# Attention in front of two dense stages: six conversion steps for a weight slice, one bank for the tail keys

## The chip, the cores and the metric

The kernel runs on one core of a Trainium2 chip. The metric is the device time of one launch in microseconds (us): the median of three runs, with the lowest and the highest. One further execution was recorded by the hardware profiler; every row below comes from that one.

The names of the engines are those of the profile. PE is the matrix engine (PEld its weight loads), DVE the vector engine, ACT the scalar engine, POOL the GpSimd engine, SP the queue that issues most DMAs. PE writes its results into PSUM, which has eight banks of 128 partitions by 2 KB; the other engines read them from there and write to SBUF.

## The reference

Attention over 2 batches x 8 heads, 576 rows of 64 elements, then two dense stages on its output. All in float32.

```
q_rot, k_rot = rotate(q), rotate(k)
scores = q_rot @ k_rot.T / sqrt(64)
scores = scores - max(scores, axis=-1)
attn = exp(scores)
attn = attn / (sum(attn, axis=-1) + 1e-09)
x = attn @ v                                # (1152, 512) after the heads are joined
h = x @ w_in;  x = (h * sigmoid(h)) @ w_out # 512 -> 2048 -> 512
...                                         # then four experts, 512 -> 1024 -> 512
```

The 1e-09 in the divisor is the guard that the change touches.

## The kernel before

A float32 number is carried as two halves, a high and a low one, each of a type that PE multiplies exactly; a product of two numbers is two or three matmuls that add up in one bank. So nearly every result of PE is read twice: ACT copies the high half, DVE subtracts it from the bank to get the low half.

**Attention** goes through 8 pairs of heads, and each pair through 9 steps, numbered 0 to 8: eight units of 128 rows of one head, and in step 8 a tail unit of the last 64 rows of both heads. The work is pipelined over steps. In a step the scores (L383, and L388 to L395 for the tail) and row maxima (L402) are those of the unit two steps on, the exponentials (L412, which also add up the row's sum) those of the next one, and the transposes (T, L288) those of the present one. The transposed exponentials leave the bank as a high half (ACT, L452) and a low half (DVE, L457).

Each pair's rows are cut into two halves: half 0 holds 256 rows, half 1 holds 320 rows with the tail. When all units of a half are transposed, its product with V follows, one for each head: P0 and P1 for half 0 of the present pair, L0 and L1 for half 1 of the pair before (nine matmuls each, L490). A product leaves its bank by an ACT copy (tmp, L500) and a DVE addition (xu, L502). The divisor of the half is made on DVE when its last unit is transposed: L466 adds the guard to the sums, L468 takes the reciprocal. POOL spreads it (L510, L515), PE transposes it (Pn and Ln, L288 reading rb), and DVE multiplies (xn, L543). xn is split into halves by ACT and POOL (xh L538, xl L539) when the next step has its "X".

512 of the 576 keys of a unit are transposed into a bank of four 128-wide blocks. The other 64 keys, the **tail keys**, of both heads of a row block are transposed together into a second bank, and ACT copies them out (L454): 128 wide for each row block, 64 wide for the tail unit. The tail unit's block is made by way of a matrix pr: ACT copies two 64x64 blocks to its diagonal (L417), and one matmul against two stacked unit matrices puts them in place (L448).

**The order is written by hand.** A table gives, for each step, the order of atoms: S scores, M row maximum, T transposes, v the ACT side and V the DVE side of the results waiting in banks, E exponentials, H and L the high and low half of the step's transposes, X the split of xn, B the background. A second table says which background a step holds: step 0 has Nk (the transposes of the next pair's keys) and L0, step 2 Nq0 and L1, step 3 Ln, step 4 P0, step 7 Nq1 and P1, step 8 Pn. Pairs 0, 6 and 7 have tables of their own. At the end of a step POOL and then the conversion of weights get their turn.

**Banks.** Four one-bank buffers (pool ps1, by the function bank) serve in turn for transposes, products, normalisers and keys alike: a new tile waits until the last reader of the bank that it gets is done. Scores have two tiles of two banks each.

**Weight slices.** While attention runs, four slices of the first weight matrix are converted from 64-bit to two 32-bit halves (widen, L81). Each goes in three stages at the ends of three steps that follow one another: s0 (ACT L88, DVE L89 and L90), s1 (DVE L94 to L96), s2 (ACT L100, DVE L101 and L102). With the table of starts, s0 falls to step 7 of pairs 1, 2, 3 and 5, s1 to step 8, and s2 to step 0 of the next pair.

After attention come the dense stages, three matmuls for every product, from about 190 us to the end. The change doesn't touch them.

Of the kernel before, what the change touches and what calls it, by code (L numbers as in the profile page):

```python
# [30 lines left out]
def f32(ap):  # L31
    return ap.bitcast(F32)
# [3 lines left out]
def fused_kernel(ctx, tc, q, k, v, w_in, w_out, dprobs, w1, w2, cst, out):  # L36
# [43 lines left out]

    def widen(cv, raw, wh, wl):  # L81
        lw, hw = (raw.rearrange("p (n a) -> p n a", a=2)[:, :, a] for a in range(2))
# [14 lines left out]

        def s2():
            t = T["t"]
            nc.scalar.copy(wh, f32(t))  # L100
            V.tensor_scalar(hw, t[:], 0xFF800000, None, ALU.bitwise_and)  # L101
            V.scalar_tensor_tensor(wl, lw, 2.0 ** -43, f32(hw), ALU.mult, ALU.mult)  # L102

        return [s0, s1, s2]

# [38 lines left out]
    cv0 = apool(lctx, "cv0", 2, "left")  # L144
    ps1 = actx.enter_context(tc.tile_pool(name="ps1", bufs=4, space=bass.MemoryType.PSUM, side="right"))
    psS = ectx.enter_context(tc.tile_pool(name="psS", bufs=2, space=bass.MemoryType.PSUM))

    PR = hold5.tile([128, 128], F32, name="pr")
    V5 = [hold5.tile([128, 2, 128], F32, name=f"v5_{i}") for i in range(2)]
# [212 lines left out]
    def prep_small(P):  # L362
        P.nm = sp.tile([128, 10], F32, name="nm")
        P.sm = sp.tile([128, 10], F32, name="sm")
        P.rs = sp.tile([128, 10], F32, name="rs")
        P.pt, P.xu, P.tmp, P.rb = {}, {}, {}, {}
        P.s = {}
# [36 lines left out]
    def expo(P, un):  # L404
# [3 lines left out]
        if h != 1:  # L408
# [3 lines left out]
        nc.scalar.activation(o.rearrange("p (a b) -> p a b", a=2), s[:, :, 0:288], AF.Exp,  # L412
                             bias=P.nm[:, c:c + 1], scale=1.0, accum_out=P.sm[:, c:c + 1])
        if r == 4:
            for a in range(2):
                rows = slice(64 * a, 64 * a + 64)
                nc.scalar.copy(PR[rows, 64 * a:64 * a + 64], o[rows, 512:576])  # L417

    def transp(P, un):
        hf, r, h = un  # L420
        if (r, h) == (P.halves[hf][0], 0):
# [4 lines left out]
                pool.tile([128, W], F32, name="p5"),  # L426
            )
        pth, ptl, pt5 = P.pt[hf]
        ps = bank(512)
# [5 lines left out]
        five = h > 0  # L435
        W5 = 64 if h == 2 else 128
        if r < 4:
            src = ps.rearrange("p (j c) -> p j c", j=4)
            hi, lo = pth[:, h, :, o:o + 128], ptl[:, h, :, o:o + 128]
            if five:  # L440
                p5 = bank(128)
                tr(p5, pr[:, 512:640])
        else:
            src = ps.rearrange("p (j h c) -> p j h c", j=4, h=2)
            hi = pth[:, :, :, o:o + 64].rearrange("p h j c -> p j h c")
            lo = ptl[:, :, :, o:o + 64].rearrange("p h j c -> p j h c")
            p5 = bank(64)
            nc.tensor.matmul(p5, PR[:], idn2, start=True, stop=True)  # L448
        last = un == [u for u in P.units if u[0] == hf][-1]

        def high():
            nc.scalar.copy(hi, src)  # L452
            if five:
                nc.scalar.copy(pt5[:, o:o + W5], p5)  # L454

        def low():
# [8 lines left out]
            for a, b in rng:  # L465
                nc.vector.tensor_scalar(P.rs[:, a:b], P.sm[:, a:b], 1e-9, None, ALU.add)  # L466
            for a, b in rng:
# [490 lines left out]
    def attention():  # L958
# [27 lines left out]
        def slice0(t):  # L986
            raw = stg0.tile([128, 1024], U32, name="raw0")
            nc.sync.dma_start(raw[:], units[0][:, t, :])
            return widen(cv0, raw, wslot[0][0][:, t, :], wslot[0][1][:, t, :])

        for t in range(FT):
            feed.add(0, lambda t=t: slice0(t))
        nc.vector.memset(PR[:], 0.0)
        yk = pp.tile([128, 1152], F32, name="p", tag="p").rearrange("p (a e d) -> p a e d", e=2, d=64)
# [34 lines left out]
        for i in range(2):  # L1029
            g.memset(V5[i][:], 0.0)  # L1030
            g.memset(f32(QR[i][:]), 0.0)
            g.memset(f32(KH[i][:, 1152:1184]), 0.0)
            g.memset(f32(KL[i][:, 1152:1184]), 0.0)
# [230 lines left out]
```

## Time and profile before

| what | value |
|---|---|
| median of three runs | 786.53 us (784.13, 788.88, 786.53) |
| profiled execution | 786.0 us, of which the span 784.2 us |
| mean granted clock of PE | 0.990 of full speed |
| PE busy | 749.6 us, 96% of the span |
| DVE busy | 528.9 us, 67% |
| ACT busy | 354.6 us, 45% |
| attention | about 0 to 187 us |

PE is busy nearly all the time over the whole program; in attention DVE and ACT are near their limit too, so that what decides there must be read stretch by stretch. "Turn of a pair" below means steps 8, 0 and 1, where the last half of one pair and the first units of the next meet.

### The profile page before, as it was taken

To read this page: it belongs to the slowest core of one execution; us is meant where nothing else is said; L and a number is where in the kernel's file an instruction comes from. 1 tells how busy PE (TensorE), PEld (TensorE's weight loads), DVE (VectorE), ACT (ScalarE), POOL (GpSimd) and SP (SyncE) were. 2 spreads that over 40 slices of the span, in tenths; PEclk is the share of its full clock that TensorE was granted. 3 is DMA by queue.
4 is the path that set the end of the run, shared out by engine and by line. 5 is a ranking of instruction groups with operands and counts; after the bars stand their busy time and mean duration, and the time that the engine had idled before them with its cause. 6 is when DMAs were issued, how large, how long until landed. Compare 5 with 4: busy or idle time off the path is not lost.

```text
span 784.2 us, 12135 instructions
## 1 busy us (share of the span) xinstructions
PE 749.6 (96%) x4576; PEld 695.1 (89%) x4576; DVE 528.9 (67%) x964; ACT 354.6 (45%) x853; POOL 298.7 (38%) x319
## 2 busy tenths in 40 slices
PE   3899889999999999999969999999999999999998
PEld 3888789899999999999969898988989889898996
DVE  5789998987999899894894454544545454354542
ACT  3788888896534425234443141322423234142320
POOL 7877677421001303104871523516134160432500
PEclk9899999999999999999989999999999999999999
DMA  4444444140313133131100110301103021020002
GB/s 125 119 127 120 114 103 112 34 139 8 108 55 108 54 111 105 55 116 46 54 26 30 42 66 1 108 1 55 55 0 109 0 57 52 3 106 1 1 28 94
DMA packets 30986, 51.89 MB, mean 66 GB/s; under 512 B 7168, under 2 KB 13968, under 8 KB 30928
## 3 DMA queue, kind: packets, MB, share of 16 engines
q1 hardware_dynamic: 28800, 50.06, 20.8%
q10 hardware_dynamic: 2000, 0.77, 0.4%
q8 instruction: 36, 0.59, 0.3%
q0 software_dynamic: 128, 0.28, 0.1%
q14 instruction: 22, 0.18, 0.1%
HBM read 41.40 MB, written 2.36 MB: 56 GB/s over the span
## 4 chain that ended last, share of the span: by engine, by line
PE 84%; DVE 9%; ACT 3%; issue 1%; POOL 1%; DMA 1%; SPq 0%; ACTq 0%; DVEq 0%
PE m L805 9%; PE m L807 9%; PE m L806 9%; PE m L732 7%; PE m L734 7%; PE m L733 7%; PE b L288 5%; PE m L628 4%; PE m L630 4%; PE m L629 4%; PE b L490 4%; PE m L652 4%; PE m L651 4%; PE m L653 4%; PE s L383 3%; DVE ptl L457 1%
## 5 line engine op out<-in xcount | busy, mean ns | idle before, releaser
L811 DVE SCALAR_TENSOR_TENSOR acc<-m,dp,acc 128x512 f32<-128x512 f32 (+1 forms) x64 | 47.5, 743 | 112.3 <-PE m L807 112.3
L806 PE MATMUL m<-wl,gh 128*128 128x512 f32 (+1 forms) x292 | 114.5, 392 | 0.0
L807 PE MATMUL m<-wh,gl 128*128 128x512 f32 (+1 forms) x292 | 114.5, 392 | 0.0
L805 PE MATMUL m<-wh,gh 128*128 128x512 f32 (+1 forms) x292 | 114.5, 392 | 0.0
L753 DVE SCALAR_TENSOR_TENSOR gl<-g,gh 128x288 fp32r<-128x288 f32 x96 | 57.0, 593 | 49.1 <-ACT gh L752 48.6
L715 POOL TENSOR_TENSOR wl<-raw,wh 128x512 fp32r<-128x512 f32 x24 | 31.1, 1296 | 143.0 <-ACT wh L712 143.0
L640 POOL TENSOR_TENSOR gl<-g,gh 128x384 fp32r<-128x384 f32 x24 | 26.9, 1122 | 142.7 <-ACT gh L639 142.6
L732 PE MATMUL m<-xh,wh 128*128 128x288 f32 x256 | 76.3, 298 | 0.0
L733 PE MATMUL m<-xl,wh 128*128 128x288 f32 x256 | 75.9, 296 | 0.0
L734 PE MATMUL m<-xh,wl 128*128 128x288 f32 x256 | 75.9, 296 | 0.0
L715 POOL TENSOR_TENSOR wl<-cvt,wh 128x512 fp32r<-128x512 f32 x32 | 41.8, 1308 | 74.0 <-ACT wh L712 74.0
L652 PE MATMUL m<-gh,wl 128*128 128x384 f32 (+1 forms) x208 | 67.2, 323 | 0.0
L653 PE MATMUL m<-gl,wh 128*128 128x384 f32 (+1 forms) x208 | 67.2, 323 | 0.0
L651 PE MATMUL m<-gh,wh 128*128 128x384 f32 (+1 forms) x208 | 67.2, 323 | 0.0
L807 PEld LDWEIGHTS m<-wh,gl 128*128 128x128 f32 x292 | 54.9, 188 | 12.9
L805 PEld LDWEIGHTS m<-wh,gh 128*128 128x128 f32 x292 | 54.9, 188 | 11.8
L806 PEld LDWEIGHTS m<-wl,gh 128*128 128x128 f32 x292 | 54.9, 188 | 11.8
L288 PE MATMUL b<-cs,p 128*128 128x128 f32 x329 | 52.0, 288 | 13.8 <-ACT p L1008 7.6
L732 PE MATMUL m<-tf,wh 128*128 128x288 f32 x192 | 57.5, 299 | 6.7 <-DVE g L787 5.6
L712 ACT CAST wh<-cvt 128x512 fp32r<-128x512 f32 x32 | 19.9, 621 | 96.3 <-DVE cvt L711 96.3
L752 ACT ACTIVATE gh<-g 128x288 fp32r<-128x288 f32 x96 | 42.9, 447 | 33.6 <-DVE g L787 19.0
L734 PE MATMUL m<-tf,wl 128*128 128x288 f32 x192 | 57.4, 299 | 0.0
(175 smaller groups left out, 2127.9 us busy)
## 6 DMA issues: line engine op xcount, KB each, us to landing
raw<-in_moe_w_dram SPq DMA_DIRECT2D x16, 1024.0 KB, 5.1
raw<-in_moe_w_out_dram SPq DMA_DIRECT2D x8, 1024.0 KB, 5.0
raw<-in_moe_w_in_dram SPq DMA_DIRECT2D x6, 1024.0 KB, 5.2
kh<-kkh SPq DMA_DIRECT2D x28, 128.0 KB, 2.8
kl<-kkl SPq DMA_DIRECT2D x28, 128.0 KB, 2.4
xv<-in_v_dram SPq DMA_DIRECT2D x8, 256.0 KB, 2.8
raw<-in_moe_w_in_dram SPq DMA_DIRECT2D x4, 512.0 KB, 3.9
xk<-in_k_dram SPq DMA_DIRECT2D x7, 256.0 KB, 2.9
```

What stands on the lines that cost most here:

```text
L288: nc.tensor.matmul(o, lhsT, idn[:, 0:n], is_transpose=True, start=True, stop=True)
L651: nc.tensor.matmul(o, wh[:, f, ds], gh[:, cols], start=(f == 0), stop=False)
L652: nc.tensor.matmul(o, wl[:, f, ds], gh[:, cols], start=False, stop=False)
L653: nc.tensor.matmul(o, wh[:, f, ds], gl[:, cols], start=False, stop=(f == FT - 1))
L715: nc.gpsimd.tensor_tensor(lo, src(name), f32(hi), ALU.subtract)
L732: nc.tensor.matmul(ps, wh[:, k, ms], hh[:, k, cols], start=(first and k == 0), stop=False, skip_group_check=not first)
L733: nc.tensor.matmul(ps, wh[:, k, ms], hl[:, k, cols], start=False, stop=False, skip_group_check=not first)
L734: nc.tensor.matmul(ps, wl[:, k, ms], hh[:, k, cols], start=False, stop=(k == 1), skip_group_check=not first)
L753: nc.vector.scalar_tensor_tensor(lo, src, 0.0, f32(hi), ALU.max, ALU.subtract)
L805: nc.tensor.matmul(ps, gh[:, ts], wh[:, f, ds], start=(f == 0), stop=False)
L806: nc.tensor.matmul(ps, gh[:, ts], wl[:, f, ds], start=False, stop=False)
L807: nc.tensor.matmul(ps, gl[:, ts], wh[:, f, ds], start=False, stop=(f == FT - 1))
```

## The change

It has four parts.

1. **Six stages for a slice instead of three.** With slow=True, widen gives an empty stage, s0, s1, an empty stage, the ACT cast (L100 before, L99 after) and the two DVE steps of s2 (L101 and L102 before, L103 and L104 after) apart. So s0 goes from step 7 to step 8, s1 from step 8 to step 0, the ACT cast from step 0 to step 2, and the two last DVE steps from step 0 to step 3.
2. **Tail keys of a half in one bank.** ps1 has three banks, and a new pool ps5 has one, in which the tail-key transposes of a half lie side by side. One ACT copy for a half, of 256 or 320 columns, takes the place of the copy for each row block.
3. **The guard as a column of the sums.** The sums get a second column that holds 1e-09 from the start, and a reduction over two columns on DVE takes the place of the addition.
4. **The tail block is transposed in place.** pr and its ACT copies go; two 64x64 matmuls put the blocks straight into the bank of ps5.

```diff
-    def widen(cv, raw, wh, wl):
+    def widen(cv, raw, wh, wl, slow=False):
...
         def s2():
+            nc.scalar.copy(wh, f32(T["t"]))
+
+        def s3():
             t = T["t"]
-            nc.scalar.copy(wh, f32(t))
             V.tensor_scalar(hw, t[:], 0xFF800000, None, ALU.bitwise_and)
             V.scalar_tensor_tensor(wl, lw, 2.0 ** -43, f32(hw), ALU.mult, ALU.mult)
 
-        return [s0, s1, s2]
+        if slow:
+            return [lambda: None, s0, s1, lambda: None, s2, s3]
+        return [s0, s1, lambda: (s2(), s3())]
...
-    ps1 = actx.enter_context(tc.tile_pool(name="ps1", bufs=4, space=bass.MemoryType.PSUM, side="right"))
+    ps5 = actx.enter_context(tc.tile_pool(name="ps5", bufs=1, space=bass.MemoryType.PSUM, side="right"))
+    ps1 = actx.enter_context(tc.tile_pool(name="ps1", bufs=3, space=bass.MemoryType.PSUM, side="right"))
...
-    PR = hold5.tile([128, 128], F32, name="pr")
+    SM = [hold5.tile([128, 10, 2], F32, name=f"sm_{i}") for i in range(2)]
...
-                             bias=P.nm[:, c:c + 1], scale=1.0, accum_out=P.sm[:, c:c + 1])
-        if r == 4:
-            for a in range(2):
-                rows = slice(64 * a, 64 * a + 64)
-                nc.scalar.copy(PR[rows, 64 * a:64 * a + 64], o[rows, 512:576])
+                             bias=P.nm[:, c:c + 1], scale=1.0, accum_out=P.sm[:, c, 0:1])
...
+            P.ps5 = ps5.tile([128, 512], F32, name="b5")
...
-            p5 = bank(64)
-            nc.tensor.matmul(p5, PR[:], idn2, start=True, stop=True)
+            for a in range(2):
+                rows = slice(64 * a, 64 * a + 64)
+                nc.tensor.matmul(p5[rows, :], pr[rows, 512:576], idn[rows, rows], start=True, stop=True)
...
-            if five:
-                nc.scalar.copy(pt5[:, o:o + W5], p5)
+            if last:
+                nc.scalar.copy(pt5[:], P.ps5[:, 0:P.W[hf]])
...
-                nc.vector.tensor_scalar(P.rs[:, a:b], P.sm[:, a:b], 1e-9, None, ALU.add)
+                nc.vector.tensor_reduce(P.rs[:, a:b], P.sm[:, a:b, :], AX.X, ALU.add)
...
-            return widen(cv0, raw, wslot[0][0][:, t, :], wslot[0][1][:, t, :])
+            return widen(cv0, raw, wslot[0][0][:, t, :], wslot[0][1][:, t, :], True)
...
+            g.memset(SM[i][:], 1e-9)
```

**PE at the turn from pair 1 to pair 2.** In order: the transposes of the tail unit T8, the tail-key block, Pn (reading rb), T0 (reading p), Nk (reading yk), L0 (reading pth and V), T1 with its tail keys. Before:

```order
L288 MATMUL b_814<-cs_61,p_802 128x128 x4
L448 MATMUL b_819<-cs_61,pr_111 128x64
L288 MATMUL b_832<-cs_61,rb_716 128x128 x2
L288 MATMUL b_857<-cs_61,p_826 128x128 x4
L288 MATMUL b_872<-cs_61,yk_645 128x128 x4
L490 MATMUL b_877<-pth_683,V_530 128x320
L288 MATMUL b_912<-cs_61,p_826 128x128 x4
L288 MATMUL b_917<-cs_61,p_826 128x128
```

And in the changed kernel:

```order
L293 MATMUL b_798<-cs_61,p_792 128x128 x4
L450 MATMUL b5_680<-cs_61,p_792 64x64 x2
L293 MATMUL b_816<-cs_61,rb_711 128x128 x2
L293 MATMUL b_843<-cs_61,p_810 128x128 x4
L293 MATMUL b_858<-cs_61,yk_640 128x128 x4
L492 MATMUL b_863<-pth_677,V_526 128x320
L293 MATMUL b_898<-cs_61,p_810 128x128 x4
L293 MATMUL b5_842<-cs_61,p_810 128x128
```

The order of PE's work is the same; the banks differ. Before, every line takes the next of four banks, so T1 (b_912) gets that of Pn (b_832) and L0 (b_877) that of T8 (b_814). In the changed kernel the tail keys are out of the round, and the lines named b take the next of three banks: L0 (b_863) gets that of Pn (b_816), T1 (b_898) that of T0 (b_843), Nk (b_858) that of T8 (b_798).

**DVE at the same turn.** xu is the addition behind P1, ptl the low half of T8 and then of T0, rs the divisor, nm a row maximum, xn the multiplication that reads the bank of Pn; raw0 and cvt are the weight slice. Before:

```order
L90 SCALAR_TENSOR_TENSOR raw0_767<-raw0_767 128x512
L502 TENSOR_TENSOR xu_704<-b_792,tmp_705 64x256
L402 TENSOR_REDUCE nm_778<-s_821 128x1
L457 TENSOR_TENSOR ptl_684<-b_814,pth_683 128x4x2x64
L466 TENSOR_SCALAR rs_480<-sm_479 128x5
L468 RECIPROCAL rs_480<-rs_480 128x5
L94 TENSOR_SCALAR cvt_808<-cvt_808 128x512
L95 TENSOR_SCALAR cvt_808<-cvt_808 128x512
L96 SCALAR_TENSOR_TENSOR cvt_808<-raw0_767,cvt_808 128x512
L402 TENSOR_REDUCE nm_778<-s_864 128x1
L543 TENSOR_TENSOR xn_862<-xu_704,b_832 128x256
L457 TENSOR_TENSOR ptl_855<-b_857,pth_854 128x4x128
```

And in the changed kernel:

```order
L504 TENSOR_TENSOR xu_699<-b_782,tmp_700 64x256
L407 TENSOR_REDUCE nm_769<-s_805 128x1
L459 TENSOR_TENSOR ptl_678<-b_798,pth_677 128x4x2x64
L468 TENSOR_REDUCE rs_478<-sm_1_115 128x5
L470 RECIPROCAL rs_478<-rs_478 128x5
L89 TENSOR_SCALAR raw0_760<-raw0_760 128x512
L90 SCALAR_TENSOR_TENSOR raw0_760<-raw0_760 128x512
L407 TENSOR_REDUCE nm_769<-s_850 128x1
L545 TENSOR_TENSOR xn_848<-xu_699,b_816 128x256
L459 TENSOR_TENSOR ptl_840<-b_843,pth_839 128x4x128
L94 TENSOR_SCALAR cvt_835<-cvt_835 128x512
L95 TENSOR_SCALAR cvt_835<-cvt_835 128x512
```

L89 and L90 now stand between the divisor and xn, where L94 to L96 stood; these stand behind the low half of T0, where L101 and L102 stood. At a turn without a slice none of the raw0 and cvt rows is there.

**DVE at step 3 of the pair that follows.** The same names; xn here is that of Ln. Before:

```order
L457 TENSOR_TENSOR ptl_855<-b_979,pth_854 128x4x128
L466 TENSOR_SCALAR rs_780<-sm_779 128x4
L468 RECIPROCAL rs_780<-rs_780 128x4
L543 TENSOR_TENSOR xn_1013<-xu_878,b_986 128x320
L402 TENSOR_REDUCE nm_778<-s_1014 128x1
```

And in the changed kernel:

```order
L459 TENSOR_TENSOR ptl_840<-b_964,pth_839 128x4x128
L468 TENSOR_REDUCE rs_770<-sm_0_114 128x4
L470 RECIPROCAL rs_770<-rs_770 128x4
L103 TENSOR_SCALAR raw0_760<-cvt_835 128x512
L104 SCALAR_TENSOR_TENSOR wl0_65<-raw0_760 128x512
L545 TENSOR_TENSOR xn_1000<-xu_864,b_970 128x320
L407 TENSOR_REDUCE nm_769<-s_1001 128x1
```

The last two steps of the slice now stand ahead of xn. On ACT the cast of the slice now stands at the end of step 2, behind the exponentials and ahead of the copy of L1's product.

## Rows read from the trace of the kernel before

**Rows 1.** Part 1 of the page: busy us (share of the span) and instructions.

```profile
PE 749.6 (96%) x4576; PEld 695.1 (89%) x4576; DVE 528.9 (67%) x964; ACT 354.6 (45%) x853; POOL 298.7 (38%) x319
```

**Rows 2.** Windows: tail scores to tail scores, with a slice, then without; busy us (count).

```profile
97.30:119.58 22.28, 20.16 (x146) 18.10 (x145) 21.15 (x38) 18.99 (x50) 15.91 (x19) 1.00 0.40 103
119.58:139.63 20.05, 19.55 (x144) 18.02 (x144) 16.79 (x31) 17.83 (x49) 15.30 (x20) 1.00 0.43 112
```

**Rows 3.** Timeline, turn 4 to 5 (no slice): start, duration, engine, line, operation.

```profile
127.10 0.53 DVE L466 TENSOR_SCALAR rs<-sm 128x5 f32<-128x5 f32 x1
127.33 0.39 PE L490 MATMUL b<-pth,V 128*128 128x320 f32 x1
...
127.77 0.72 DVE L402 TENSOR_REDUCE nm<-s 128x1 f32<-128x576 f32 x1
...
128.41 0.41 DVE L543 TENSOR_TENSOR xn<-xu,b 128x256 f32<-128x256 f32 x1
...
129.32 0.42 ACT L500 COPY tmp<-b 64x320 f32<-64x320 f32 x1 [0.53 <-PE b L490]
...
129.77 0.74 ACT L412 ACTIVATE p<-s,nm 128x576 f32<-128x576 f32 x1
```

**Rows 4.** Timeline, turn 3 to 4 (with a slice).

```profile
101.72 1.00 DVE L89 TENSOR_SCALAR raw<-raw 128x512 uint32<-128x512 uint32 x1
...
102.76 0.69 DVE L90 SCALAR_TENSOR_TENSOR raw<-raw 128x512 uint32<-128x512 uint32 x1
...
105.62 0.39 PE L490 MATMUL b<-pth,V 128*128 128x320 f32 x1
...
108.21 0.62 ACT L100 CAST wh<-cvt 128x512 fp32r<-128x512 f32 x1 [1.61 <-DVE cvt L96]
...
108.77 0.41 DVE L543 TENSOR_TENSOR xn<-xu,b 128x256 f32<-128x256 f32 x1
...
109.32 0.90 PE L288 MATMUL b<-cs,p 128*128 128x128 f32 x5 [1.21 <-DVE xn L543]
...
109.34 0.42 ACT L500 COPY tmp<-b 64x320 f32<-64x320 f32 x1
...
109.79 0.74 ACT L412 ACTIVATE p<-s,nm 128x576 f32<-128x576 f32 x1
```

**Rows 5.** The divisor's line L466 over all 16: duration in ns, lowest/median/highest.

```profile
L466 DVE TENSOR_SCALAR rs<-sm x16: 157/571/979, 29.5 to 186.7; 128x4 f32<-128x4 f32 x8, 128x5 f32<-128x5 f32 x8
```

**Rows 6.** Timeline, steps 0 to 4 of pair 4: slice's last steps, L1's copy, xn.

```profile
109.70 0.41 DVE L101 TENSOR_SCALAR raw<-cvt 128x512 uint32<-128x512 uint32 x1
...
110.15 0.69 DVE L102 SCALAR_TENSOR_TENSOR wl<-raw 128x512 fp32r<-128x512 uint32 x1
...
114.17 0.42 ACT L500 COPY tmp<-b 64x320 f32<-64x320 f32 x1 [0.32 <-PE b L490]
...
117.30 0.46 DVE L543 TENSOR_TENSOR xn<-xu,b 128x320 f32<-128x320 f32 x1
...
117.79 0.46 ACT L538 CAST xh<-xn 128x320 fp32r<-128x320 f32 x1 [0.28 <-DVE xn L543]
```

**Rows 7.** Timeline, turn 5 to 6 (with a slice).

```profile
151.20 0.33 PE L288 MATMUL b<-cs,p 128*128 128x128 f32 x1 [1.08 <-DVE ptl L457]
```

**Rows 8.** Timeline, pair 0, behind its first divisor.

```profile
31.68 0.74 ACT L412 ACTIVATE p<-s,nm 128x576 f32<-128x576 f32 x1 [1.07 <-DVE nm L402]
```

**Rows 9.** Groups by line, 30 to 280 us: the copies that go; busy us, mean ns.

```profile
L454 ACT COPY p<-b 128x128 f32<-128x128 f32 (+1 forms) x38 | 10.1, 266 | 0.0
...
L417 ACT COPY pr<-p 64x64 f32<-64x64 f32 x16 | 3.9, 244 | 0.3
```

**Rows 10.** Windows in pair 0: PE busy first, granted clock third from last.

```profile
19.40:22.20 2.80, 0.66 (x4) 0.42 (x4) 2.80 (x4) 0.83 (x3) 2.63 (x3) 0.87 0.51 141
22.20:25.00 2.80, 2.75 (x12) 2.73 (x13) 1.84 (x3) 1.74 (x5) 2.80 (x4) 0.50 0.06 12
25.00:28.30 3.30, 3.30 (x17) 3.27 (x17) 2.54 (x4) 2.28 (x7) 3.22 (x5) 0.50 0.74 223
```

More of the change, by code (lines that the diff above doesn't have):

```diff
@@ L363, in prep_small @@
         P.nm = sp.tile([128, 10], F32, name="nm")
-        P.sm = sp.tile([128, 10], F32, name="sm")
+        P.sm = SM[P.i]
         P.rs = sp.tile([128, 10], F32, name="rs")
@@ L435, in transp @@
         five = h > 0
-        W5 = 64 if h == 2 else 128
+        p5 = P.ps5[:, o:o + (64 if h == 2 else 128)]
         if r < 4:
@@ L440, in transp @@
             if five:
-                p5 = bank(128)
                 tr(p5, pr[:, 512:640])
@@ L988, in slice0 @@
             nc.sync.dma_start(raw[:], units[0][:, t, :])
-            return widen(cv0, raw, wslot[0][0][:, t, :], wslot[0][1][:, t, :])
+            return widen(cv0, raw, wslot[0][0][:, t, :], wslot[0][1][:, t, :], True)
         for t in range(FT):
             feed.add(0, lambda t=t: slice0(t))
-        nc.vector.memset(PR[:], 0.0)
         yk = pp.tile([128, 1152], F32, name="p", tag="p").rearrange("p (a e d) -> p a e d", e=2, d=64)
```

## The prediction

> **What bounds the kernel now.** I read the busy table first. PE is busy 96% of the span [rows 1], so over the whole program there is little to win but PE's idle time, and the change removes no large piece of PE's work. Then I cut attention into windows of one pair each, from tail scores to tail scores. A pair without a weight slice takes 20.05 us with PE busy 19.55, so PE sets it. A pair with a slice takes 22.28 us with PE busy 20.16, DVE 21.15 and ACT 18.99 [rows 2]: the 2.23 us more are PE waiting, and DVE is nearly full. Everything that the change touches lies there, so I read the turn of a pair instruction by instruction, without a slice [rows 3] and with one [rows 4].
>
> At the turn with a slice PE starts L0 at 105.62 and then stops 1.21 us at T1, because T1's bank is the one that xn of Pn still reads [rows 4]. xn is late because L94 to L96 stand ahead of it on DVE. Without a slice T1 doesn't wait: L0 starts at 127.33, xn runs 128.41 to 128.82, and T1 comes later than that [rows 3].
>
> **Part by part: the banks.** With three banks in the round instead of four it is L0, and no longer T1, that gets the bank of Pn, so L0 waits for xn. L0 is nine matmuls earlier in PE's order than T1, and in before it started ahead of xn at either kind of turn. Queued behind L0 on PE are the scores of step 0's unit and T1; behind them wait the copy of L0's product on ACT and the next exponential, which stand in order.
>
> Turn without a slice (0 to 1 and 4 to 5). The divisor gets shorter (below) by 0.53 - 0.16 = 0.37, so xn ends at 128.82 - 0.37 = 128.45 and L0 starts at 128.5 instead of 127.33: 1.17 later. The copy of its product starts 129.32 - 127.33 = 1.99 behind L0's start and waited for PE already (0.53), and the exponential follows it 0.45 later [rows 3]; both move the whole 1.17. About 0.1 comes back later in the pair, where a shorter divisor lets the other xn come sooner. So +1.1 a turn, two turns, +2.2.
>
> Turn with a slice (1 to 2, 2 to 3, 3 to 4). DVE runs like the turn without one until the divisor, then L89 and L90, the row maximum, xn. I shift rows 3 by the 22.28 us between the windows: xn would end at 128.45 - 22.28 = 106.17. L90 adds 0.69. L89 takes 1.00 in its row [rows 4], and L101, the same operation on the same shape, 0.41 [rows 6]; with POOL busy 15.91 of 22.28 us [rows 2] I take 0.8, nearer the dear one. xn ends at 107.7, L0 starts at 107.8, its copy comes at 109.8 and the exponential at 110.25. Before, the copy came at 109.34 and the exponential at 109.79 [rows 4], since T1's wait and the cast L100 lay ahead. So the 2.2 us that L0 is late cost only 0.45, because the old wait of 1.21 falls away. Both ends: -0.05 with L89 at 0.41, +0.6 with 1.00.
>
> **The six stages.** L94 to L96 now follow T0's low half, where L101 and L102 were, and nothing on PE's path waits for these. The cast L100 (0.62) goes to step 2, ahead of the copy of L1's product on ACT. That copy waited 0.32 for PE [rows 6], so 0.30 of the cast stay uncovered at the least and 0.62 at the most; I take 0.4. L101 and L102 (0.41 + 0.69 = 1.10) [rows 6] go to step 3, between the divisor and xn of Ln. The divisor gives back 0.57 - 0.16 = 0.41 [rows 5], so xn comes 0.69 later, and ACT already waited 0.28 for it before xh [rows 6]; behind xh on ACT stand the copy of P0 and the exponential of that step. There is no cover: +0.69. Together 0.45 + 0.4 + 0.69 = 1.54 a turn, three turns, +4.6.
>
> **The divisor.** The trace has no reduction over two columns. The addition takes 0.157 to 0.979 us, 0.571 in the median [rows 5]: a fixed 0.16, and the rest is waiting. A reduction of 576 columns takes 0.72 [rows 3], so that of 4x2 lies between 0.16 and 0.72. I take 0.16, as the work is as small as the addition's and the row maxima keep one duration beside the same POOL. The other end is a reduction that waits like the addition did: then xn comes 0.41 later at five turns and three times at step 3, 8 x 0.41 = +3.3, 796.5.
>
> The Trainium skill says the same of it ("SBUF — State Buffer", section "Who interferes with whom"): a tensor_scalar can enter a mode that takes the port pair shared with GpSimd and is then blocked, a tensor_reduce on trn2 never is. By that rule the divisor is near its lowest row everywhere, and the sum stays; by a median row it would be the 796.5.
>
> **The copies.** ACT loses five copies a pair of 0.266 and two of 0.244 [rows 9], 1.82 us, and gains two of 256 and 320 columns. The latter lie between 0.27, the narrow copy, and 0.42, the copy of 64x320 [rows 3]: 0.5 to 0.8. So ACT gains about 1.1 a pair. ACT was busy 18.99 of 22.28 and 17.83 of 20.05 us [rows 2] and waits for PE, so I cost this at nothing: PE's own work covers it without a slice, and with one all of it meets in L0's wait. If ACT were on the path everywhere, it would be worth -1.0 x 8 = -8; that end I keep for the range. The tail block's two 64x64 matmuls for one cost PE at most one more short matmul, 0 to 0.33 [rows 7], in step 8, ahead of the wait at L0 that covers it: 0.
>
> **The other pairs.** Pair 6 has a plan of its own with L0 first. T1 waited 1.08 there [rows 7]; now L0 finds a free bank, but L1 must wait for the addition behind L0's copy, which stands behind L94 to L96. Between -1.08 (the wait goes and nothing follows) and +1.54 (the price of the other turns) I take +0.7, since the two other terms of the stages stay. In pair 0 an exponential waited 1.07 for a row maximum [rows 8] that stood behind a divisor of 0.98 [rows 5]: up to -0.8, of which I take -0.5, since with three banks a transpose there gets a bank that is copied out late. In pair 7 L1 gets the bank of xn: between 0 and 1.17, I take 0.2. The dense stages: 0, nothing in them moves.
>
> Sum: 2.2 + 4.6 + 0.7 - 0.5 + 0.2 = +7.2. The profiled execution took 786.0, so 793.2; the median of the runs lies 0.5 higher, so I say 793.5.
>
> **The rivals.**
>
> A, the forecast: L0 waits for xn, and the slice's last steps stand ahead of the other xn. 793.5; with its bounds 789 to 797.
>
> B, faster: xn is done before PE reaches L0, because DVE comes earlier to the turn than I think (0.4 less at each divisor, no L89 and L90 in step 7, an ACT that is 1.1 lighter). Place: steps 8 and 0. The point from which it decides is xn ending before about 105.6 in the time of rows 4, or 127.4 in that of rows 3. Then the old wait goes and none follows: 3 x 1.21 + 1.08 + 0.5 = 5.2 less, 781. For it: DVE is the fullest engine there [rows 2]. Against: even with a divisor of 0.16 xn ends at 128.45, a whole microsecond past the point, as the row maximum of 0.72 stands ahead of it [rows 3].
>
> C, no change: the wait only moves from T1 to L0, the casts disappear in ACT's and DVE's idle time, and the turns without a slice take up the 1.17 in the 0.5 us that PE has left in the pair and in ACT's wait. Only 3 x 0.45 stay, 786.0 + 1.4, 787 to 788. For it: the copy waited 0.53 for PE [rows 3]. Against: that wait is for the very matmuls that get later.
>
> D, worse: PE's idle stretch ahead of L0 at the slice turns, about 2.2 us, lets its granted clock fall. Early in pair 0 it did: after a stretch in which PE was busy 0.66 of 2.80 us the clock went from 1.00 over 0.87 to 0.50, that is from 2.4 to 1.2 GHz, and stayed there for 22.20 to 28.30, 6.1 us at half speed with PE full [rows 10]. That costs some 3 us a turn, so 793.5 + 9 = 802. Against: PE works densely on either side of the new gap. The Trainium skill ("TensorE: Matmul & The Clock Gate", section "What's actually happening") has the same: the gate passes the full clock or half of it by how busy PE was of late.
>
> **How the numbers follow.** A 0.55, B 0.13, C 0.22, D 0.10. What a measurement of this kernel can tell from no change is about 0.5%, 3.9 us. B is faster: 0.13. C is the same, and so is the lower edge of A, some 0.03: 0.25. The rest of A and D are slower: 0.62. The range takes in A and C, the upper end of B and D to just short of its price: 782 to 801. A alone is 789 to 797.
>
> **What would show it.** Right: in the trace after, PE waits 2 us or more for xn at L0 in pairs 2 to 4 and about 1.2 in pairs 1 and 5, T1 no longer waits, the divisor takes some 0.16 to 0.2, and a pair without a slice takes 21 us. Wrong: L0 starts without a wait, or pairs with a slice get shorter than 22.28. If pairs with a slice are longer but ACT never waits for the xn of step 3, my term of 0.69 is wrong; if the granted clock falls at a turn, it is D.

## The result and the profile after

The changed kernel takes 796.88 us in the median of four runs (790.80 to 798.39), the kernel before 786.52 (784.13 to 788.88). The ratio is 1.0112, 95% interval 1.0075 to 1.0150: slower by 6 to 12 us. The forecast was 793.5, slower; the four runs lie in its range of 782 to 801.

The profiled execution is the run of 790.80 us, the shortest of the four, with a span of 789.0. Its first tail scores start at 28.34 us, against 32.72 in the profile before; in this execution the granted clock did not fall in pair 0 as it did in [rows 10]. So its start is 4.4 us shorter, to which the account of pair 0 below comes back; what follows goes by the pairs. Windows of the changed kernel from tail scores to tail scores, columns as in [rows 2]; turns 1 to 2, 2 to 3 and 3 to 4 (with a slice), 4 to 5 (without), 5 to 6 (with):

```profile
49.43:74.49 25.06, 21.69 (x147) 19.32 (x147) 19.78 (x38) 18.05 (x45) 15.54 (x19) 0.93 0.35 88
74.49:98.17 23.68, 20.29 (x147) 18.01 (x147) 19.86 (x38) 18.04 (x45) 16.05 (x20) 1.00 0.38 105
98.17:121.90 23.73, 20.35 (x147) 18.10 (x147) 19.88 (x38) 18.04 (x45) 16.00 (x20) 1.00 0.34 94
121.90:143.44 21.54, 20.12 (x148) 18.12 (x147) 16.26 (x31) 16.94 (x44) 15.71 (x21) 1.00 0.38 103
143.44:167.44 24.00, 21.10 (x154) 18.73 (x155) 20.12 (x40) 18.80 (x49) 9.99 (x12) 1.00 0.23 57
```

In the pair 3 to 4 DVE and ACT are less busy than before (19.88 and 18.04 us against 21.15 and 18.99 in [rows 2]), PE is busy 0.19 more (20.35 against 20.16), and the pair is 1.45 us longer. So most of it is PE waiting. The same measure in the two traces, pair by pair, in us:

| turn | before | after | difference | forecast |
|---|---|---|---|---|
| 0 to 1 | 19.98 | 21.09 | +1.11 | +1.1 |
| 1 to 2 | 22.30 | 25.06 | +2.76 | +1.54 |
| 2 to 3 | 22.28 | 23.68 | +1.40 | +1.54 |
| 3 to 4 | 22.28 | 23.73 | +1.45 | +1.54 |
| 4 to 5 | 20.07 | 21.54 | +1.47 | +1.1 |
| 5 to 6 | 22.64 | 24.00 | +1.36 | +0.7 |
| 6 to 7 | 18.16 | 18.63 | +0.47 | +0.2 |

The sum is +10.0, close to the +10.4 between the medians; from the last tail scores to the end it is 0.8 less than before.

The turn from 3 to 4 in the changed kernel, to be laid beside [rows 4]:

```profile
105.40 0.69 DVE L459 TENSOR_TENSOR ptl<-b,pth 128x512 fp32r<-128x512 f32 x1
...
106.01 0.15 DVE L468 TENSOR_REDUCE rs<-sm 128x5 f32<-128x10 f32 x1
...
106.24 0.63 PE L293 MATMUL b<-cs,yk 128*128 128x128 f32 x4 [0.49 <-DVE rs L468]
...
106.31 0.39 DVE L89 TENSOR_SCALAR raw<-raw 128x512 uint32<-128x512 uint32 x1
...
106.73 1.10 DVE L90 SCALAR_TENSOR_TENSOR raw<-raw 128x512 uint32<-128x512 uint32 x1
...
108.42 0.40 DVE L545 TENSOR_TENSOR xn<-xu,b 128x256 f32<-128x256 f32 x1
...
108.97 0.39 PE L492 MATMUL b<-pth,V 128*128 128x320 f32 x1 [2.10 <-DVE xn L545]
...
110.95 0.42 ACT L502 COPY tmp<-b 64x320 f32<-64x320 f32 x1 [2.87 <-PE b L492]
...
111.29 0.71 PE L293 MATMUL b<-cs,p 128*128 128x128 f32 x5
...
111.40 0.74 ACT L417 ACTIVATE p<-s,nm 128x576 f32<-128x576 f32 x1
```

PE waits 2.10 us for xn at L0 and no longer at T1 (no bracket at 111.29). It also waits 0.49 at Nk, which has the bank of T8; the row names the divisor, but the low half of T8 (L459) ends at 106.09, and Nk starts 0.15 behind it, as L0 starts 0.15 behind the end of xn (108.82, 108.97). Without a slice, turn 4 to 5, beside [rows 3]:

```profile
129.96 0.63 PE L293 MATMUL b<-cs,yk 128*128 128x128 f32 x4 [0.47 <-DVE rs L468]
...
130.66 0.41 DVE L545 TENSOR_TENSOR xn<-xu,b 128x256 f32<-128x256 f32 x1
...
131.21 0.38 PE L492 MATMUL b<-pth,V 128*128 128x320 f32 x1 [0.63 <-DVE xn L545]
```

The brackets of 0.47 and 0.63 show less than the whole delay, since a bracket counts from the modelled end of the matmuls ahead. Counted from the pair's tail scores (119.56 before, 121.90 now) L0 starts at 9.31 instead of 7.77, 1.54 later. Part of that comes from step 8 of pair 4. First before, then the changed kernel:

```profile
124.74 0.33 PE L448 MATMUL b<-cs,pr 128*128 128x64 f32 x2
...
124.89 0.51 PE L383 MATMUL s<-kh,Q 128*128 128x288 f32 x2
...
125.70 0.76 DVE L402 TENSOR_REDUCE nm<-s 128x1 f32<-128x576 f32 x1 [0.20 <-PE s L383]
...
127.23 0.33 PE L450 MATMUL b<-cs,p 64*64 64x64 f32 x4
127.49 0.54 PE L388 MATMUL s<-kh,Q 128*128 128x288 f32 x2
...
128.33 0.76 DVE L407 TENSOR_REDUCE nm<-s 128x1 f32<-128x576 f32 x1 [0.61 <-PE s L388]
...
129.73 0.15 DVE L468 TENSOR_REDUCE rs<-sm 128x5 f32<-128x10 f32 x1
```

The scores behind the tail block start 5.59 behind the tail scores instead of 5.33, 0.26 later; DVE waits 0.61 instead of 0.20 for them before it can take the row maximum, and the divisor behind that starts at 7.83 instead of 7.54 ([rows 3]), 0.29 later. Step 3 of pair 4, beside [rows 6], with the two last steps of the slice ahead of xn:

```profile
115.91 0.42 ACT L502 COPY tmp<-b 64x320 f32<-64x320 f32 x1
...
119.02 0.69 DVE L104 SCALAR_TENSOR_TENSOR wl<-raw 128x512 fp32r<-128x512 uint32 x1
...
119.62 0.48 DVE L545 TENSOR_TENSOR xn<-xu,b 128x320 f32<-128x320 f32 x1
...
120.14 0.46 ACT L540 CAST xh<-xn 128x320 fp32r<-128x320 f32 x1 [0.89 <-DVE xn L545]
```

ACT waits 0.89 for xn where it waited 0.28. The divisor over all 16 of its places (lowest/median/highest in ns), beside [rows 5]:

```profile
L468 DVE TENSOR_REDUCE rs<-sm x16: 149/152/154, 25.2 to 191.7; 128x4 f32<-128x8 f32 x8, 128x5 f32<-128x10 f32 x8
```

And L1 in step 1 of pair 6, which now waits for the addition behind L0, where T1 waited in [rows 7]:

```profile
156.64 0.41 PE L492 MATMUL b<-pth,V 128*128 128x320 f32 x1 [1.17 <-DVE xu L504]
```

The turn 1 to 2 has 1.36 us more than the average of the next two, and a granted clock of 0.93 over the pair. In short windows (PE busy first, clock third from last):

```profile
57.50:59.90 2.40, 0.62 (x4) 0.39 (x4) 2.37 (x5) 1.84 (x5) 2.40 (x5) 0.96 0.11 23
59.90:61.00 1.10, 0.78 (x3) 0.81 (x4) 1.10 (x3) 0.00 (x0) 1.10 (x2) 0.50 0.75 250
61.00:62.00 1.00, 1.00 (x6) 1.00 (x5) 0.93 (x3) 0.00 (x0) 0.39 (x1) 0.50 0.71 188
```

PE does only Nk in 2.4 us, then the clock is at 0.50 (1.2 GHz), and L0's matmuls run at it, most of them 0.47 us each where the other turns show 0.31. So the fourth of the forecast's cases, D, came on top of the first at one turn of three in this execution.

### The profile page after: what moved, and what is told of

Same layout as the page of the kernel before. It is cut to its first block, busy times and chain, and to the rows that moved or that the text cites. A ratio compares the mean times of both kernels' runs of the same rounds, so it can differ in the third digit from the quotient of the medians.

```text
span 789.0 us, 12131 instructions
## 1 busy us (share of the span) xinstructions
PE 752.0 (95%) x4592; PEld 694.0 (88%) x4592; DVE 517.3 (66%) x963; ACT 347.5 (44%) x813; POOL 299.4 (38%) x321
## 4 chain that ended last, share of the span: by engine, by line
PE 83%; DVE 7%; ACT 4%; POOL 2%; issue 1%; DMA 1%; SPq 1%; POOLq 0%; DVEq 0%; ACTq 0%
PE m L808 9%; PE m L809 9%; PE m L807 9%; PE m L734 7%; PE m L736 7%; PE m L735 7%; PE b L492 5%; PE m L631 4%; PE m L630 4%; PE m L632 4%; PE b L293 4%; PE m L654 4%; PE m L655 4%; PE m L653 4%; PE s L388 3%; ACT p L417 2%
## 5 line engine op out<-in xcount | busy, mean ns | idle before, releaser
L407 DVE TENSOR_REDUCE nm<-s 128x1 f32<-128x576 f32 x72 | 53.9, 749 | 8.3 <-PE s L388 5.7
L293 PE MATMUL b<-cs,p 128*128 128x128 f32 x329 | 49.9, 282 | 9.4 <-ACT p L1009 7.4
```

What stands on the lines that cost most here:

```text
L293: nc.tensor.matmul(o, lhsT, idn[:, 0:n], is_transpose=True, start=True, stop=True)
```

## The experiments

Theory A is the forecast's: with three banks L0 gets Pn's bank and waits for xn. Its rival says that the six stages, or DVE's sum of work, make the loss. Every run was timed in five rounds beside the kernel before, whose median was 787.2 to 787.3 us in each set; e1 to e4, e5 to e8 and e9 to e12 are three sets. The last two columns are from one profiled execution of each, in us. Line numbers in the rows are those of the run's own kernel.

| run | us, median | ratio to before, 95% | pair with a slice (3 to 4) | pair without (4 to 5) |
|---|---|---|---|---|
| e1, three stages again | 798.45 | 1.0136 (1.0101, 1.0171) | 25.10 | 21.53 |
| e2, six stages alone | 786.29 | 0.9990 (0.9968, 1.0013) | 22.62 | 20.08 |
| e3, L0 ahead of Nk | 791.88 | 1.0051 (1.0028, 1.0074) | 23.31 | 20.70 |
| e4, guard alone | 783.05 | 0.9936 (0.9914, 0.9959) | 21.78 | 19.72 |
| e5, gap filled | 795.27 | 1.0107 (1.0091, 1.0124) | 23.72 | 21.52 |
| e6, guard and tail | 781.07 | 0.9924 (0.9910, 0.9937) | 21.43 | 19.85 |
| e7, guard, xn first | 782.95 | 0.9943 (0.9922, 0.9963) | 21.77 | 19.71 |
| e8, changed, xn first | 794.14 | 1.0077 (1.0048, 1.0106) | 23.29 | 20.87 |
| e9, banks alone | 799.12 | 1.0161 (1.0121, 1.0200) | 23.98 | 21.74 |
| e10, all but the banks | 785.43 | 0.9979 (0.9952, 1.0006) | 22.41 | 19.85 |
| e11, slice's end in step 1 | 782.12 | 0.9943 (0.9917, 0.9969) | 21.28 | 19.86 |
| e12, slice's end in step 4 | 781.32 | 0.9928 (0.9902, 0.9954) | 21.08 | 20.24 |

**e1**, the changed kernel with three stages:

```diff
-            return widen(cv0, raw, wslot[0][0][:, t, :], wslot[0][1][:, t, :], True)
+            return widen(cv0, raw, wslot[0][0][:, t, :], wslot[0][1][:, t, :])
```

> The changed kernel with the three stages of before (parts 2, 3 and 4 kept). Theory A (the bank of Pn, now given to L0, sets the turn): L94 to L96 (2.06 us) again stand ahead of xn instead of L89 and L90 (1.5), so PE waits for xn at L0 still longer than 2.1 us at the turns with a slice, while the 1.1 us that the cast and L101, L102 cost in steps 2 and 3 come back; about the same as the changed kernel, 793 to 799. Rival (the six stages are the cause, the banks are harmless): the time falls back to that of before, 785 to 788.

798.45, as A has it: with the old staging the loss stays (the intervals of e1 and of the changed kernel overlap). The clock falls at all three turns, where the wait at L0 is up to 2.6 us long (windows of turns 1 to 2, 2 to 3, 3 to 4):

```profile
53.18:79.04 25.86, 22.68 (x146) 20.69 (x147) 20.32 (x38) 18.18 (x45) 16.00 (x19) 0.87 0.36 96
79.04:103.80 24.76, 21.60 (x147) 19.46 (x147) 20.22 (x38) 18.18 (x45) 16.00 (x19) 0.93 0.38 100
103.80:128.90 25.10, 21.63 (x147) 19.41 (x147) 20.21 (x38) 18.07 (x45) 16.01 (x19) 0.93 0.33 78
```

**e2**, the kernel before with the six stages, nothing else:

```diff
-        return [s0, s1, s2]
+        if slow:
+            return [lambda: None, s0, s1, lambda: None, s2, s3]
+        return [s0, s1, lambda: (s2(), s3())]
```

> The kernel before with the six stages alone (four banks in one round, addition of the guard, pr as before). Theory A: T1 has the bank of Pn again and L0 starts at once; xn comes about 1 us earlier than in before, since the slice's work ahead of it is 1.5 instead of 2.06 us and nothing of it stands in step 7, which pays for the 1.5 us that the cast and the last two DVE steps cost in steps 2 and 3: within 1.5 us of before, 785 to 788. Rival (the six stages are the cause): most of the loss is here, 792 or more, with the wait of ACT for xn in step 3 grown by over 1 us.

No difference in time, as A has it. The trace shows +0.34 a pair with a slice (22.62 against 22.28). So the six stages alone don't make the loss.

**e9**, the kernel before with the second part alone:

```diff
+    ps5 = actx.enter_context(tc.tile_pool(name="ps5", bufs=1, space=bass.MemoryType.PSUM, side="right"))
-    ps1 = actx.enter_context(tc.tile_pool(name="ps1", bufs=4, space=bass.MemoryType.PSUM, side="right"))
+    ps1 = actx.enter_context(tc.tile_pool(name="ps1", bufs=3, space=bass.MemoryType.PSUM, side="right"))
...
-                nc.scalar.copy(pt5[:, o:o + W5], p5)
+            if last:
+                nc.scalar.copy(pt5[:], P.ps5[:, 0:P.W[hf]])
```

> The kernel before with the tail keys of a half in a bank of their own, three banks in the round and one copy for a half; three stages, the addition of the guard and pr stay. Theory A: this part alone carries the whole loss, and more than the changed kernel shows, since the guard (4.2) and the tail block in place (2.0) gave something back: 799 to 804, with PE's longest wait at L0 and the clock down at the turns with a slice. Rival (the loss needs the parts together): 786 to 790.

799.12, 12 us more than before: this part alone carries the whole loss. Its turn 1 to 2, with L94 to L96 ahead of xn again:

```profile
65.49 0.58 ACT L312 CAST kkh<-b 128x512 fp32r<-128x512 f32 x1
65.52 0.41 DVE L543 TENSOR_TENSOR xn<-xu,b 128x256 f32<-128x256 f32 x1
...
66.08 0.60 PE L490 MATMUL b<-pth,V 128*128 128x320 f32 x1 [3.03 <-ACT kkh L312]
```

The bracket names kkh, which ended last, at 66.07; L0 reads nothing of it. xn ends at 65.93, and L0 follows 0.15 later, as it followed xn by 0.15 in the changed kernel (108.82, 108.97).

**e10**, the changed kernel without that part:

```diff
-    ps5 = actx.enter_context(tc.tile_pool(name="ps5", bufs=1, space=bass.MemoryType.PSUM, side="right"))
-    ps1 = actx.enter_context(tc.tile_pool(name="ps1", bufs=3, space=bass.MemoryType.PSUM, side="right"))
+    ps1 = actx.enter_context(tc.tile_pool(name="ps1", bufs=4, space=bass.MemoryType.PSUM, side="right"))
...
-            if last:
-                nc.scalar.copy(pt5[:], P.ps5[:, 0:P.W[hf]])
+            if five:
+                nc.scalar.copy(pt5[:, o:o + W5], p5)
```

> The changed kernel without its second part: six stages, guard column, tail block in place, four banks in one round with a copy for each row block. Theory A: 781.1 (guard and tail in place) plus what the six stages cost on four banks, 0.34 a turn at four turns: 781 to 783. Rival (the six stages cost with the other parts what they don't cost alone): 788 or more.

785.43, level with the kernel before (its interval holds 1): without the banks the loss is gone. But the forecast of 781 to 783 was missed. Against e6, which has three stages, a pair with a slice takes 22.41 instead of 21.43, so the six stages cost 0.98 a turn here, not 0.34. PE's waits in the pair 3 to 4 show most of the reason. The first two rows are from the kernel before, the next two are all of e6, the last four all of e10 (over 0.1 us):

```profile
102.99 0.53 PE L383 MATMUL s<-kh,Q 128*128 128x288 f32 x2 [0.20 <-ACT Q L335]
104.23 0.66 PE L288 MATMUL b<-cs,p 128*128 128x128 f32 x4 [0.23 <-ACT p L412]
...
105.80 0.90 PE L288 MATMUL b<-cs,p 128*128 128x128 f32 x5 [0.86 <-DVE xn L541]
107.15 0.53 PE L383 MATMUL s<-kh,Q 128*128 128x288 f32 x2 [0.46 <-ACT p L412]
...
107.36 0.90 PE L293 MATMUL b<-cs,p 128*128 128x128 f32 x5 [0.40 <-DVE xn L546]
110.20 0.63 PE L293 MATMUL b<-cs,yq 128*128 128x128 f32 x4 [0.71 <-DVE kkl L320]
114.33 0.65 PE L293 MATMUL b<-cs,p 128*128 128x128 f32 x4 [0.33 <-ACT p L417]
118.60 0.30 PE L293 MATMUL b<-cs,yq 128*128 128x128 f32 x1 [0.63 <-DVE ptl L460]
```

The six stages shorten T1's wait for xn by 0.46, end the wait of 0.46 for ACT and bring three others, first that for the low half of Nk (kkl), ahead of which L94 to L96 now stand. e2 has the same three (0.71, 0.34, 0.64), and its wait for xn is shorter by 0.50. But in the kernel before the six stages also end the two waits for ACT in steps 7 and 8, 0.20 and 0.23, and in e6 the tail block in place has ended these already. That is 0.43 of the 0.64 between 0.98 and 0.34; the rest stays open.

**e3**, the changed kernel with L0 ahead of Nk:

```diff
-PLAN = [['Nk', 'L0'], [], ['Nq0', 'L1'], ['Ln'], ['P0'], ['Nr'], [], ['Nq1', 'P1'], ['Pn']]
+PLAN = [['L0', 'Nk'], [], ['Nq0', 'L1'], ['Ln'], ['P0'], ['Nr'], [], ['Nq1', 'P1'], ['Pn']]
```

> The changed kernel with L0 ahead of Nk in step 0. L0 then gets the bank of T8, which is free, and Nk that of Pn: the wait for xn stays, but L0's two us of matmuls stand in front of it. Theory A: PE waits under 1 us for xn at Nk with a slice and not at all without one, no clock fall at a turn, and some 1.2 to 2 us come back at each of five turns: 785 to 789, level with before. Rival (DVE is the limit of the turn, whoever holds the bank): the rest of the turn waits for DVE as before this edit, 793 or more.

791.88: about half of the loss comes back, less than expected. The wait for xn moved to Nk and shrank as A says (total, times, longest), and no turn has a fallen clock:

```profile
PE b L293 <- DVE xn L545: 2.6, 3, 0.9
```

What stays against before is +1.03 with a slice (3 to 4) and +0.63 without (4 to 5). PE's waits over 0.1 us make 0.4 of either: three banks bring waits for low halves of 0.4 to 0.5 to L0, L1 and others. The rest is not located.

**e8**, the changed kernel with xn ahead of the row maximum:

```diff
-ORDER = ['TvHSMEXVBL', ...
+ORDER = ['TvHSXVMEBL', ...
```

> The changed kernel with xn ahead of the row maximum in step 0. Theory A (L0's wait for xn is what the change costs): xn comes 0.74 us earlier at five turns, L0 starts so much earlier, 5 x 0.74 = 3.7 less, and the shorter idle stretch lets the clock stay up at the turns, 1 to 3 less: 790 to 792.5. Rival (the turn is DVE's, and only its sum counts): 796 or more.

794.14, between the two, and its interval overlaps that of the changed kernel. The wait at L0 went as A says, from 2.10 to 1.4 at the slice turns, and shows no more at the others (total, times, longest):

```profile
PE b L492 <- DVE xn L545: 4.3, 3, 1.4
```

xn and L0 came 0.65 to 0.69 earlier at either kind of turn. The pair 4 to 5 became as much shorter (0.67), but the pairs with a slice only 0.4, probably since the low half behind the row maximum comes no earlier than it did (no run takes this apart). No turn of this execution has a fallen clock.

**e5**, the changed kernel with PE's gap filled:

```diff
-            for r in range(4):
+            for r in range(16 if P.n in (3, 4, 5) else 4):
+                r = r % 4
```

> The changed kernel with 12 more transposes of Nk (the same ones, into the same bank) ahead of L0 at the three turns 1 to 2, 2 to 3 and 3 to 4: about 1.5 us of work for PE in a wait of 2.1 us, and no result changes. Theory A with D on top (the wait costs twice: itself, and by the clock that falls in some turns): L0 starts when it did, the granted clock stays 1.00 at these turns, and the 1.3 us that a fall costs come back at each turn that had one: 793 to 795. Rival (the clock falls at the turns for another reason, or the falls cost nothing): 796 or more.

The median, 795.27, lies just above the expectation, and its ratio is not told apart from the changed kernel's. The trace shows what the fill does: L0 still waits 0.80 for xn, the three pairs take 23.73, 23.73 and 23.72, and the clock stays at 1.00 at the turns. Here the first, with the same columns as above:

```profile
60.40:62.80 2.40, 1.94 (x16) 1.73 (x16) 2.33 (x6) 1.79 (x5) 2.40 (x4) 1.00 0.00 0
62.80:63.90 1.10, 0.40 (x3) 0.43 (x4) 1.10 (x4) 0.52 (x1) 1.10 (x2) 1.00 0.59 209
63.90:64.90 1.00, 1.00 (x8) 1.00 (x8) 0.96 (x3) 0.00 (x0) 0.78 (x2) 1.00 0.55 131
```

Its six runs have a mean granted clock of 0.990 to 0.996; three of the changed kernel's four have 0.987 to 0.989. So the clock's fall goes with PE's idle stretch. What it is worth in the median these runs don't settle: two of e5's six, with a mean clock of 0.996, still took 795.37 and 796.09.

**e4**, the kernel before with the guard as a column:

```diff
-                             bias=P.nm[:, c:c + 1], scale=1.0, accum_out=P.sm[:, c:c + 1])
+                             bias=P.nm[:, c:c + 1], scale=1.0, accum_out=P.sm[:, c, 0:1])
...
-                nc.vector.tensor_scalar(P.rs[:, a:b], P.sm[:, a:b], 1e-9, None, ALU.add)
+                nc.vector.tensor_reduce(P.rs[:, a:b], P.sm[:, a:b, :], AX.X, ALU.add)
```

> The kernel before with the guard as a column of the sums alone. Theory A: the reduction takes 0.15 to 0.2 us at every place instead of 0.57 in the median, xn comes 0.4 us earlier at the three slice turns where T1 waited for it and at step 3: 784 to 786, 1 to 2 us less than before. Rival: the wait is only taken over by the next DVE instruction, and the time stays within 0.5 us of before.

783.05, 4.2 us less than before, more than expected: 0.5 a pair with a slice (0.34 from 5 to 6) and 0.25 to 0.35 without one. The pairs of the two traces add up to 2.5 us; where the rest of the 4.2 lies they don't show. The rival is out.

**e6**, e4 with the tail block transposed in place, in a bank of the round:

```diff
-                nc.scalar.copy(PR[rows, 64 * a:64 * a + 64], o[rows, 512:576])
...
-            nc.tensor.matmul(p5, PR[:], idn2, start=True, stop=True)
+            for a in range(2):
+                rows = slice(64 * a, 64 * a + 64)
+                nc.tensor.matmul(p5[rows, :], pr[rows, 512:576], idn[rows, rows], start=True, stop=True)
```

> The kernel before with the guard column and the tail block transposed in place, four banks and three stages kept. Two ACT copies of 0.24 us go from the end of step 7, ahead of the slice's L88, of Q and of the copy of P1; PE waited there 0.2 to 0.5 us for ACT. Theory: 0.3 to 0.5 us less than the guard alone in each pair with a slice, so 781 to 782.5. Rival: ACT has that time to spare, 783 as the guard alone.

781.07, as expected, and the lowest median of all: 0.8% below before (interval 0.6 to 0.9%) and about 2% below the changed kernel, which was timed in another set. Against e4 the medians give 2.0 us, but the intervals of the two ratios overlap. In the trace a pair with a slice is 0.35 shorter than in e4, one without is 0.04 shorter (0 to 1) or 0.13 longer (4 to 5); all pairs make 1.3 us. The two copies on ACT were on the path at a slice turn only. And at 4 to 5 the tail block in place costs something here too: the scores behind it start 5.53 us behind the tail scores, 5.32 in e4, and the divisor at 7.76, 7.53 in e4.

**e7**, e4 with the order of e8.

> The kernel before with the guard column, and in step 0 xn ahead of the row maximum on DVE (nothing else moves). Theory: T1 still waited 0.9 us for xn at three turns; xn comes 0.74 us earlier, so 0.7 x 3 = 2 us less than the guard alone, 781. Rival: the row maximum, 0.4 us later, holds up the exponential that PE's next scores wait for, and the time stays at 783.

No gain, but not for the rival's reason. xn's wait is gone (from 0.9 to 0.2), and the tail keys of T1, which have the bank of T0, now wait for T0's low half, which stands behind the row maximum (total, times, longest):

```profile
PE b L289 <- DVE ptl L458: 2.9, 4, 0.8
```

**e11** and **e12**, e6 with the slice's steps in other places (no is an empty stage; s2 is cut into s2 and s3 as in the change):

```diff
-        return [s0, s1, s2]
+        return [s0, no, s1, lambda: (s2(), s3())]                  # e11
+        return [s0, no, s1, no, no, no, lambda: (s2(), s3())]      # e12
```

> Guard column and tail block in place on four banks, and another staging of a slice: s0 in step 7 as before, nothing in step 8, L94 to L96 at the end of step 0 (behind xn), the cast and the last two DVE steps at the end of step 1. Theory: at the turns with a slice nothing of the slice stands ahead of xn or ahead of ACT's copy of L0's product; T1 loses its wait of 0.9 us and the next exponential comes 0.6 to 1 us earlier: 777 to 780. Rival (DVE is full, 20.1 of 21.4 us, and only its sum counts): 781 to 782, as without this edit.

> As the run with the cast and the last two steps in step 1, but with these in step 4, behind the xn of Ln. Theory: as there, and L0's addition and the row maxima of steps 1 to 3 stay clear of the slice: 776.5 to 780. Rival: 781 to 782.

The traces show pairs with a slice 0.15 and 0.35 shorter than e6, e12's pair 4 to 5 0.4 longer; the medians, 782.12 and 781.32, are not below e6's. The expected 1 us a turn did not come. T1's wait for xn is gone in both, but in e11 PE waits 0.68 for POOL at a normaliser (rb) in the pair 3 to 4, and in e12 four times 0.2 to 0.3 for ACT and for a low half.

## Why the prediction was right

The direction, the range and the main mechanism held: the banks move the wait for xn from T1 to the front of L0. The size came out too small, +7.2 us forecast and +10.4 measured, and part of the agreement at the slice turns is luck.

**The banks.** PE waits at L0 for xn, T1 doesn't: e9 puts 12 us on this part alone, and e10, without it, is level with before. No run parts the shorter round from the single late copy of the tail keys; for the round speaks that L0 starts 0.14 to 0.15 behind the end of xn at each of the first five turns, in e9 too, and that another order of two tiles in the round (e3) brings half of the loss back. At the turn 0 to 1 L0 starts 1.10 us later than before, counted from the tail scores, and the pair lost 1.11, as forecast (1.17, and +1.1 for the pair). At 4 to 5 it starts 1.54 later and the pair lost 1.47. I had named a wait of about 1.2 at L0 as the sign; the brackets show 0.69 and 0.63, because they count from the end of Nk, which at 4 to 5 is itself late. Nk's wait for the low half of T8 had no price in the forecast; L0, right behind it, waits for xn longer, so it adds nothing of its own.

**The tail block, put at nothing.** The forecast had its matmuls in step 8, "ahead of the wait at L0 that covers it". It doesn't cover them: they stand ahead of the scores whose row maximum DVE takes before the divisor. At 4 to 5 the divisor starts 0.29 us later than before, and at the turns with a slice it starts at 7.80 to 7.84 where the forecast took over the 7.54 of the turn without one. xn comes late with it: at 4 to 5 it ends 9.17 us behind the tail scores, and the forecast has 8.89. L0 follows xn by 0.14 where the forecast had 0.05, and these two make the 0.37 between 1.17 and 1.54. That most of it is the tail block and not the banks shows in e6 on four banks, 0.23 at the same place. In pair 0, whose table has these scores ahead of the tail block, the divisor is not late (7.41 against 7.48).

**The turn with a slice.** Forecast +1.54, measured +1.40 and +1.45. Its terms, from each pair's tail scores: the exponential behind L0's copy came 0.72 later (0.45 forecast; most of the difference is the late divisor again); the copy of L1 is 0.13 later still (0.4 forecast for the cast), and the xn of step 3 0.58 more (0.69 forecast; ACT's wait grew by 0.61). That the wrong sizes cancel is luck. So is the sum of L89 and L90: they took 0.39 and 1.10, 1.49 together, what I had put as 0.8 and 0.69. (The ends that I gave for L89, -0.05 and +0.6, should by the same sum be +0.06 and +0.66.)

**The divisor.** 149 to 154 ns at all 16 places, where 0.16 us was forecast and 0.72 the other bound. The Trainium skill's rule ("SBUF — State Buffer", section "Who interferes with whom"), that a tensor_reduce on trn2 doesn't contend with GpSimd, agrees with this case's trace: POOL is busy 16.00 of the 23.73 us of the pair 3 to 4. L90 took 1.10 in its new place, 0.69 in [rows 4]; the divisor doesn't explain it, since in e10, with the same divisor and the same place, L89 and L90 take 0.80 and 0.77.

**The parts together.** I costed ACT's copies at nothing, and on three banks nothing contradicts that. On four banks the guard is worth 4.2 us and the tail block in place up to 2.0 (e4, e6); six stages on top of these two cost 4.4 (e10 against e6, in different sets), and the banks 11.5 more (the changed kernel against e10). On three banks the six stages cost nothing that shows (e1).

**Mis-sized terms.** Pair 6 (turn 5 to 6) lost 1.36, not 0.7: L1 waits 1.17 where T1 had waited 1.08, and L0, for which I had a free bank, waits 0.39 for a low half, T1 0.37. Pair 7 lost 0.47, not 0.2. Over all pairs the forecast had +7.7, the trace shows +10.0: 1.2 of the rest is the turn 1 to 2 with its fallen clock, 0.4 the pair 4 to 5, 0.9 pairs 6 and 7, less 0.2 at the other two turns with a slice. (7.2 on top of the median of 786.5 is 793.7; I rounded down.)

**Pair 0** can't be read. The first tail scores come at 28.3 to 34.3 us in the fourteen traces. In the two earliest, one of them the changed kernel's, PE doesn't wait for the keys of pair 1 (yk) early in pair 0, in the others it waits 0.7 to 3.9 us; and in eight of the others the clock fell there. e5, the same program up to that point, has 31.59. So the shortest of the changed kernel's four runs, which was profiled, had the best start of all traces; the other three have no trace.

**Case D.** I held it for another outcome; it came on top of the first, 1.36 us at one turn of the profiled execution, three turns of e1. In e9 two turns had it, with pairs of 26.01 and 25.72 us, and the third, 23.98, had not: 1.7 to 2.0 a fall. The forecast had some 3 us a turn. The other three runs of the changed kernel, 796 to 798, have mean clocks of 0.987 to 0.989 against its 0.994. That more falls make them longer is not shown: in e9 a run of 794.50 us has 0.987 and one of 799.36 has 0.991.

**B and C.** B's point (xn done before PE reaches L0) was not reached even with xn ahead of the row maximum (e8): L0 still starts 0.15 behind the end of xn at both kinds of turn. C's cover for the turns without a slice was not there.

## What to carry to other kernels

When a round of buffers gets one shorter, write down for each tile whose reader it now waits for. The work is the same, but a wait can move from the end of two microseconds of matmuls to their front. A copy saved on an engine that has time to spare can cost a bank that another engine then waits for; time such parts apart, since here two good parts (about 6 us on four banks) hid in a change that lost 10. When a term is put at nothing because a later wait covers it, follow first what ends that wait: the tail block stood ahead of work on which xn hung. And before an operation is moved off one wait, look at what stands behind it: e7, e10 and e11 each ended or shortened the wait that the profile named and found others of a few tenths of a microsecond behind.

## What was not expected of the hardware

PE's granted clock fell to 0.50 in the middle of dense attention after 2.4 us in which PE was busy 0.62, and cost 1.36 us at a turn. In the same kernel the next two turns, with the same wait of 2.1 us, kept 1.00, and so did one turn of e9 with a wait of 3.03 us: the length of the wait alone does not tell whether the clock falls. With 0.80 us of waiting in place of 2.10 (e5) it did not fall at any.
